# An fp32 first layer by 20 block products in four PSUM banks in place of 22 in pairs of banks

## The chip, the cores and the metric

The kernel runs on one core of a Trainium2 chip. The time is device time in microseconds (us) of one launch; three runs of the kernel before gave 584.62, 584.01 and 584.42, median 584.42. Engines are named TensorE (PE, matmul; PEld is its weight load), VectorE (DVE), ScalarE (ACT), GpSimd (POOL) and SyncE (SP, which here only issues DMAs). Every engine works off its own instructions in the order in which the program wrote them.

## The reference

An RWKV-6 attention over a sequence of 768 steps, and then a two-layer network with a silu between the layers. All arrays are float32.

```python
B, H, S, D = r.shape                    # 4, 8, 768, 48
for t in range(S):
    cur = einsum('bhd,bhe->bhde', u * k[t], v[t])
    y[t] = einsum('bhd,bhde->bhe', r[t], state + cur)
    state = w[t][..., None] * state + einsum('bhd,bhe->bhde', k[t], v[t])
x = y.transpose(0, 2, 1, 3).reshape(B * S, H * D)      # 3072 x 384
h = x @ w_in                                           # w_in 384 x 2048
out = (h * sigmoid(h)) @ w_out                         # w_out 2048 x 384
```

## The kernel before

The 3072 tokens are cut into 12 units: 128 steps of two of the four batches, so a unit has 256 tokens of the network. `mix(i)` writes the attention of unit i as a list of groups of steps; the main loop walks the groups and puts after each one a number of steps of the network: the second layer of unit i - 2 (`downs`, seven products per unit by a Strassen-like scheme, called quarters here) and the first layer of unit i - 1 (`ups`). The schedule is manual: what this order says is the order on each engine's queue. After mix(11) follows a tail without attention: `downs(10)`, `ups(11)`, `downs(11)`.

Attention of a unit. `load_blocks(i, name, g)` loads a quarter of w, r or k with four small DMAs on SyncE's queue into `raw`; `turn` transposes it with VectorE; `product`, `grow_own`, `grow_keys` (GpSimd) and `grow_queries` (VectorE) build the scaled keys and queries level by level; `odd_keys` and half of `prepare` are ScalarE copies. `burst(i, l)` has TensorE make the scores of levels l and l + 1, and `keep_level` puts them into `score`: with VectorE for levels 3 and 4, with twelve ScalarE copies for levels 5 and 6. Scores inside blocks of eight steps go another way: `block_bonus` (GpSimd multiplications, steps 0 to 7) and `block_sum` (VectorE reductions, steps 0 to 4) fill `block_sums`; `block_move` sends them through DRAM (`kept`) back into `spare` in another layout, on SyncE's queue; `block_spread` copies that on ScalarE, and `block_write` writes it with two predicated copies of VectorE, each over a whole half of `score` (index e). At the unit's end `turn_apart`, `y_state`, `y_values` and `update` use `score` on TensorE, and `turns(i + 1)` transposes the next w and k. The result y goes through DRAM (`x_out`, `x_in`) into `xt`, the input of the first layer. `load_rk` loads the inputs of `block_bonus` for the next unit.

First layer, units 3 to 11. The transposed product has 2 x 3 x 2 blocks: w_in in two halves of its columns and three chunks of rows, x in three chunks of rows and two batches. 11 block products per half, made for two halves of 512 columns each (22 in all, each 8 matmuls of 64 weight columns by 128 tokens, recorded as 16 instructions), are accumulated in the banks h0, h1, o0 and o1. In the places x, y and z a product can follow a product of its place at once; the partial sums leave by `nc.scalar.copy` and come back by `nc.vector.tensor_tensor` into `gt`, not into PSUM. The sums of weights (`in_weight_sums`, four sums of 1024 columns) are made once in mix(3) and mix(4), the five sums of x per unit by `sums_of_x`. Then `sums` (L1130, VectorE) makes what the second layer needs: eight additions of 512 columns per unit.

Places. `slot` keeps w and r of the units from 4 on in slot 0 of `raw` and k in two slots by turns, so k is loaded two units ahead; slot 1 of w and r holds sums of weights from mix(3) on.

Of the kernel before, what the change touches and what calls it, by code (L numbers as in the profile page):

```python
# [38 lines left out]
def kernel(  # L39
# [59 lines left out]
    def slot(i, name):  # L99

        return 0 if i >= NPAIR and name != "k" else i % NSLOT
# [387 lines left out]
    def block_bonus(i, step):  # L489
# [3 lines left out]
        if step == 0:  # L493
            ruk[i] = pt.tile([128, 2 * W], F32, name="ruk", bufs=1)
            mul(ruk[i], at_rk(R_AT, [1, 2 * W]), at_rk(K_AT, [1, 2 * W]))
        elif step == 1:
            have = ruk[i].rearrange("p (e s d) -> p e s d", e=2, s=BLK)
            mul(have, have, u_bc[:, 0:1][:, :, None, :].to_broadcast([128, 2, BLK, D]))
# [18 lines left out]
        else:  # L517
            e = step - 6
            to = (room_b, ruk[i])[e]
            mul(to.rearrange("p (k q d) -> p k q d", k=4, q=4), at_rk(K_AT + e * W, [D, 4], [0, 4], [1, D]),  # L520
                at_rk(R_AT + e * W + 4 * D, [0, 4], [D, 4], [1, D]))
# [35 lines left out]
    def block_write(i):  # L557

        shape = [128, NB, NP, L // BLK, BLK]
        for e in range(2):  # L560
            nc.vector.copy_predicated(out=score[:, i % NSC, e].rearrange("p (b q) (i s) -> p b q i s", b=NB, s=BLK),
                                      mask=block_mask[:, :, None].to_broadcast(shape),
                                      data=block_both[:, :, e::2][:, :, :, None, :].to_broadcast(shape))
# [300 lines left out]
    p_x = {}  # L864

    def x_products(i, b):

        if b == 0:
            xt[i] = pt.tile([128, KC, TU], F32, name="xt", bufs=1)
# [53 lines left out]
    def x_in(i, queue=nc.scalar):  # L923

        xt[i] = pt.tile([128, KC, TU], F32, name="xt", bufs=1)
        queue.dma_start(out=xt[i], in_=turned[i].rearrange("h d t -> (h d) t").rearrange("(c p) t -> p c t", p=128))
# [11 lines left out]

    late = []

    def mix(i):
# [15 lines left out]
        def start(j):  # L957
            return [*[(product, j, l) for l in range(1, NL)], (grow_own, j, 1)]

        end = [[*at(i > NFAST, (sums, i - 1, 0)), *at(ahead, *bonus_steps(i + 1, 0, 1, 2, 3))],  # L960
               [*at(i < len(units) - NB, (turn_apart, i), (turn_k, i)), (y_state, i), *both(y_values, i), *at(ahead, *turns(i + 1)),
                *at(i <= NFAST, (sums, i - 1, FH // 2 - 2)), *both(update, i), *at(not ahead, (move_x, i))]]
        if i < NPAIR:
# [9 lines left out]
                      [(burst, i, 5), (keep_level, i, 5), (keep_level, i, 6), (go_on, i, 6)], *end]  # L973
        else:
            groups = [[*both(turn, i, "r"), (grow_own, i, 0), (x_out, i - 1)],
                      [*start(i), *sum_steps(i, 0, 1), *bonus_steps(i, 4, 5), (x_in, i - 1)],
                      [(odd_keys, i, 2), (grow_keys, i, 2, False), (grow_queries, i, 2), *sum_steps(i, 2)],
                      [(prepare, i, 3), *bonus_steps(i, 6, 7)],
                      [(burst, i, 3), (keep_level, i, 3), *sum_steps(i, 3, 4), (block_move, i), *at(ahead, (load_rk, i + 1))],
                      [(keep_level, i, 4), (go_on, i, 4)],  # L980
                      [(prepare, i, 5), (reverse_v, i)],
                      [(block_spread, i), (block_write, i)],
                      [(burst, i, 5), (keep_level, i, 5), (keep_level, i, 6), (go_on, i, 6)], *end]

        loads = [*at(i >= NPAIR and ahead, *block_loads(i + 1, "w")), *at(i >= NPAIR - 1 and ahead, *block_loads(i + 1, "r")),
                 *at(i + NSLOT < len(units), *block_loads(i + NSLOT, "k"))]
# [3 lines left out]
        if i == NPAIR - 1:  # L990
            late.extend(loads[-2:])
            loads = loads[:-2]
        if i == NPAIR:
            groups[1] += late
            groups[3] += loads[:2]
            loads = loads[2:]

        behind = groups[8 if i < NPAIR else 5 if i == NPAIR else 2:][:4 if i + NSLOT >= len(units) else None]
        for at, group in enumerate(behind):
            group += loads[at * len(loads) // len(behind):(at + 1) * len(loads) // len(behind)]  # L1000
# [8 lines left out]
    def up(i, m):  # L1009
        p_h = ps.tile([128, 2, TU], F32, name="p_h", bufs=2)  # L1010
        for a in range(2):
            f = 2 * m + a
            for c in range(KC):
                nc.tensor.matmul(p_h[:, a, :], lhsT=w_in_sb[:, c, f * 128:(f + 1) * 128], rhs=xt[i][:, c, :],  # L1014
                                 start=(c == 0), stop=(c == KC - 1))
# [9 lines left out]
    HALF = DF // 2  # L1025
    whole_w = raw[:, 1].rearrange("p x b h d -> p x (b h d)")
    in_sums = [whole_w[:, WRK["r"]], const.tile([128, HALF], F32, name="in_sum"), whole_w[:, WRK["w"]]]
    a11, a12, a13 = (w_in_sb[:, c, 0:HALF] for c in range(KC))
    a21, a22, a23 = (w_in_sb[:, c, HALF:DF] for c in range(KC))
    x_sums = [spare[:, at + x * L:at + (x + 1) * L] for x in range(3)] + [const.tile([128, L], F32, name="x_sum")]  # L1030

    def in_weight_sums(which):
        out, one, two, op = ((in_sums[0], a21, a22, ALU.add), (in_sums[1], in_sums[0], a11, ALU.subtract),
                             (in_sums[2], a12, in_sums[1], ALU.subtract), (a21, a11, a21, ALU.subtract))[which]
        nc.vector.tensor_tensor(out=out, in0=one, in1=two, op=op)

    def sums_of_x(i):

        (b11, b12), (b21, b22), (b31, b32) = (tuple(xt[i][:, c, b * L:(b + 1) * L] for b in range(NB)) for c in range(KC))
        d1, d2, d4, d3 = x_sums  # L1040
        for out, one, two in ((d1, b12, b11), (d2, b22, d1), (b12, b22, b12), (d4, b21, d2), (d3, b31, b32)):
            nc.vector.tensor_tensor(out=out, in0=one, in1=two, op=ALU.subtract)
# [9 lines left out]
    def first_layer(i, half, *names):  # L1052

        (b11, b12), (b21, b22), (b31, b32) = (tuple(xt[i][:, c, b * L:(b + 1) * L] for b in range(NB)) for c in range(KC))
        d1, d2, d4, d3 = x_sums
        s1, s2, s4 = in_sums
        for name in names:
            place, first, last, pairs = {
                "p1": ("x", True, True, [(a11, b11)]), "p6": ("x", False, True, [(s2, d2)]), "p7": ("x", False, True, [(a21, b12), (a23, b32)]),
                "p4": ("x", False, True, [(a22, d4), (a23, d3)]), "p5": ("y", True, True, [(s1, d1)]),  # L1060
                "p3": ("y", False, True, [(s4, b22), (a13, b32)]), "p2": ("z", True, False, [(a12, b21)]),
                "n1": ("z", False, True, [(a13, b31)])}[name]
            p = kept[{"x": ("h0", "h1"), "y": ("o0", "h0"), "z": ("o1", "o1")}[place][half]][:].rearrange("p (q t) -> p q t", q=4)
            for n, (left, right) in enumerate(pairs):
                for q in range(4):
                    for h in (0, PD):
                        f = (4 * half + q) * 128 + h
                        nc.tensor.matmul(p[h:h + PD, q, :], lhsT=left[:, f:f + PD], rhs=right, start=first and n == 0 and q == 0,  # L1068
                                         stop=last and n == len(pairs) - 1 and q == 3, skip_group_check=True)

            def g(x, b):
                if (i, x, b, half) not in gt:
                    gt[i, x, b, half] = pt.tile([128, 4, L], F32, name="gt", bufs=FC // 2)
                return gt[i, x, b, half]
# [244 lines left out]
```

## Time and profile before

| what | value |
|---|---|
| median of three runs | 584.42 us |
| span of the profiled execution | 582.4 us (the page gives no other time for it) |
| first quarter of mix(4) to the tail, eight units | 169.58 to 522.96 us |
| tail | 522.96 to 582.4 us |
| TensorE L1068, first layer (16 instructions make a block product) | 274 ns each, pipelined |
| VectorE L1080, joins of the first layer | 0.68 us each |
| VectorE L1130, sums, two SBUF operands | 0.91 and 0.70 us on average |
| VectorE L561, block_write | 1.31 to 2.93 us, mean 1.52 |
| ScalarE L1077 / L1083 / L1085, copy and silu of 512 columns | 0.58 / 0.63 / 0.59 us |
| GpSimd L491, 768 / 384 columns | 1.83 to 2.30 / 1.15 to 1.23 us |
| SyncE L127, issue of one block load | 0.45 us in the median, 0.31 to 1.9 |

Times are us from the span's start. A row of the timeline has start, duration, engine, line, operation, output <- inputs, shape and count; in brackets stands the idle time before it and what ended it. Rows with a count merge instructions that follow each other. The chain is the sequence of work and waits that ended last.

### The profile page before, as it was taken

What the parts mean: (1) busy time and instruction counts of PE and PEld (TensorE: products, weight loads), DVE (VectorE), ACT (ScalarE), POOL (GpSimd) and SP (SyncE); (2) the same over time, 40 slices, a digit from 0 to 9 for tenths busy, and PEclk for the clock granted to TensorE, in tenths of its full rate; (3) what the DMA queues carried; (4) which work ended last, traced back from release to release, by engine and by line L of the source; (5) the groups of instructions that cost most, each with busy time, mean ns of one, the idle gap of its engine ahead of it and who ended that gap; (6) DMA issues with size and microseconds to landing.
All of it is one profiled execution on the core that took longest, in us unless ns stands there. A gap on an engine that the chain in (4) does not pass through costs nothing.

```text
span 582.4 us, 19225 instructions
## 1 busy us (share of the span) xinstructions
PE 572.0 (98%) x8070; PEld 534.0 (92%) x8070; DVE 433.9 (75%) x703; ACT 264.4 (45%) x582; POOL 350.4 (60%) x415
## 2 busy tenths in 40 slices
PE   8989999999999999999999999999999999999997
PEld 7768776798899999999999999999999899999997
DVE  7979789998997787787787687697686877771150
ACT  5679694531531561561560560560471361471320
POOL 6989778447777459459457559559647847700000
PEclk9989999999999999999999999999999999999999
DMA  9957775344453544554545455545355462102000
GB/s 225 320 118 215 168 231 88 48 91 95 100 90 68 112 84 82 120 83 80 117 71 89 104 86 94 117 77 95 77 98 101 70 128 60 38 4 55 28 5 24
DMA packets 206102, 57.62 MB, mean 99 GB/s; under 512 B 185664, under 2 KB 197824, under 8 KB 206016
## 3 DMA queue, kind: packets, MB, share of 16 engines
q1 hardware_dynamic: 197904, 49.51, 42.1%
q10 hardware_dynamic: 8112, 6.88, 4.4%
q8 instruction: 63, 1.03, 0.8%
q14 instruction: 23, 0.19, 0.1%
HBM read 47.14 MB, written 9.18 MB: 97 GB/s over the span
## 4 chain that ended last, share of the span: by engine, by line
PE 81%; POOL 6%; DVE 6%; issue 3%; SPq 2%; DMA 1%; ACT 0%; DVEq 0%; POOLq 0%
PE p_o L1159 24%; PE p_h L1068 20%; PE p_o L1068 9%; PE p_h L1014 9%; PE p_h L1159 4%; PE p_m L1098 4%; PE p_sc L692 2%; POOL tk L634 2%; PE p_m L856 2%; PE p_m L835 2%; PE p_m L692 2%; SPq L127 1%; DVE score L710 1%; DMA raw<-in_r_dram 1%; POOL w_in_sb L259 1%
## 5 line engine op out<-in xcount | busy, mean ns | idle before, releaser
L634 POOL TENSOR_TENSOR tk<-tk,tw 128x256 f32<-128x256 f32 x128 | 89.8, 722 | 30.3 <-ACT tk L604 22.9
L1159 PE MATMUL p_o<-own,temps 128*128 128x192 f32 x528 | 87.9, 326 | 0.0
L1159 PEld LDWEIGHTS p_o<-own,temps 128*128 128x128 f32 x528 | 86.1, 190 | 0.1
L491 POOL TENSOR_TENSOR ruk<-tokens_rk 128x768 f32<-128x768 f32 (+1 forms) x32 | 54.3, 1707 | 44.8 <-DMA tokens_rk<-in_k_dram 35.2
L406 POOL TENSOR_TENSOR tw<-tw 128x256 f32<-128x256 f32 (+6 forms) x83 | 39.3, 473 | 54.4 <-DVE tw L360 50.5
L1014 PE MATMUL p_h<-xt,w_in_sb 128*128 128x256 f32 x288 | 67.8, 391 | 0.8 <-POOL w_in_sb L259 0.6
L1014 PEld LDWEIGHTS p_h<-xt,w_in_sb 128*128 128x128 f32 x288 | 54.7, 194 | 9.3 <-POOL w_in_sb L259 1.1
L1068 PE MATMUL p_h<-xt,w_in_sb 128*64 128x128 f32 x1008 | 62.0, 274 | 0.0
L616 DVE TENSOR_TENSOR tr<-tr,tw 128x512 f32<-128x512 f32 x61 | 58.1, 953 | 3.0 <-PE p_m L692 2.5
L1159 PE MATMUL p_o<-w_out_sb,gt 128*128 128x192 f32 x340 | 60.0, 329 | 0.3 <-DVE temps L1130 0.2
L1159 PEld LDWEIGHTS p_o<-w_out_sb,gt 128*128 128x128 f32 x340 | 55.3, 190 | 1.5 <-DVE temps L1130 0.5
L1068 PEld LDWEIGHTS p_h<-xt,w_in_sb 128*64 128x64 f32 x1008 | 55.3, 137 | 1.3 <-issue 0.2
L604 ACT COPY tk<-tk 128x256 f32<-128x256 f32 x52 | 21.2, 407 | 76.0 <-POOL tk L634 62.6
L1068 PE MATMUL p_o<-xt,w_in_sb 128*64 128x128 f32 x720 | 47.0, 273 | 0.0
L1164 ACT COPY partial<-p_o 128x192 f32<-128x192 f32 x33 | 10.5, 319 | 78.5 <-PE p_o L1159 72.7
L1068 PEld LDWEIGHTS p_o<-xt,w_in_sb 128*64 128x64 f32 x720 | 40.9, 137 | 0.0
L1077 ACT COPY gt<-p_h 128x512 f32<-128x512 f32 x45 | 26.2, 583 | 31.1 <-PE p_h L1068 31.1
L710 DVE COPY_PREDICATED score<-mask,p_sc 128x512 f32<-128x512 int8 x42 | 31.3, 800 | 9.5 <-PE p_sc L692 9.2
L1083 ACT ACTIVATE gt<-gt 128x512 f32<-128x512 f32 x36 | 22.7, 631 | 31.6 <-DVE gt L1080 31.2
L525 DVE TENSOR_REDUCE block_sums<-ruk 128x4 f32<-128x192 f32 (+1 forms) x48 | 24.2, 546 | 15.0 <-POOL ruk L491 15.0
L1080 DVE TENSOR_TENSOR gt<-p_o,gt 128x512 f32<-128x512 f32 x27 | 18.5, 684 | 20.0 <-PE p_o L1068 20.0
L1159 PE MATMUL p_o<-w_out_sb,temps 128*128 128x192 f32 x176 | 30.4, 326 | 0.0
(225 smaller groups left out, 1236.3 us busy)
## 6 DMA issues: line engine op xcount, KB each, us to landing
w_out_sb<-in_moe_w_in_dram SPq DMA_DIRECT2D x6, 768.0 KB, 6.7
w_out_sb<-in_moe_w_out_dram SPq DMA_DIRECT2D x4, 768.0 KB, 5.0
own<-in_moe_w_out_dram SPq DMA_DIRECT2D x4, 768.0 KB, 5.7
tokens_rk<-in_r_dram SPq DMA_DIRECT2D x8, 384.0 KB, 4.5
tokens_rk<-in_k_dram SPq DMA_DIRECT2D x8, 384.0 KB, 5.3
tokens_w<-in_w_dram SPq DMA_DIRECT2D x8, 384.0 KB, 6.8
turned<-yt ACTq DMA_DIRECT2D x16, 192.0 KB, 2.7
xt<-turned ACTq DMA_DIRECT2D x8, 384.0 KB, 3.3
```

The costliest lines, as they stand in the source:

```text
L406: engine.tensor_tensor(out=up, in0=t[:, :, 0::2], in1=t[:, :, 1::2], op=ALU.mult)
L491: mul = lambda out, one, two: nc.gpsimd.tensor_tensor(out=out, in0=one, in1=two, op=ALU.mult)
L525: add = lambda out, have: nc.vector.tensor_reduce(out=out, in_=have, axis=mybir.AxisListType.X, op=ALU.add)
L616: nc.vector.tensor_tensor(out=odd, in0=odd, in1=tw[i][l][:, :, 0::2][:, :, :, None].to_broadcast([128, Q, L >> (l + 1), c]), op=ALU.mult)
L634: nc.gpsimd.tensor_tensor(out=out, in0=have, in1=odd_products(i, l, b, *blocks), op=ALU.mult)
L692: nc.tensor.matmul(to, lhsT=tk[i][rows, X[l % 2] + p, x * 64:(x + 1) * 64], rhs=have, start=True, stop=True)
L710: nc.vector.copy_predicated(out=dst, mask=masks[l][:, :, None].to_broadcast([128, NB, NP, ni, c]), data=sc[e].rearrange("p (b q) (i c) -> ...
L1014: nc.tensor.matmul(p_h[:, a, :], lhsT=w_in_sb[:, c, f * 128:(f + 1) * 128], rhs=xt[i][:, c, :], start=(c == 0), stop=(c == KC - 1))
L1068: nc.tensor.matmul(p[h:h + PD, q, :], lhsT=left[:, f:f + PD], rhs=right, start=first and n == 0 and q == 0, stop=last and n == len(pairs) ...
L1077: nc.scalar.copy(out=g(*{"p1": (0, 0), "p6": (0, 1), "p5": (1, 1)}[name]), in_=p)
L1098: nc.tensor.matmul(po[i, b], lhsT=gt[i, f // 2][:, f % 2, b * L:(b + 1) * L], rhs=w_out_sb[:, f, :], start=(f == 0), stop=(f == FC - 1))
L1159: nc.tensor.matmul(p, lhsT=left(f), rhs=right[:, f, :], start=which in (0, 1, 3) and f == 0, stop=f == FH - 1, skip_group_check=True)
```

## The change

The first layer from unit 3 on is cut finer: w_in in four quarters of 512 columns, so the product has 4 x 3 x 2 blocks, and 20 block products in place of 22 give it. Each of four banks holds a running sum. Between products the content of a bank is copied to another bank or to `gt`, or joined with such a copy and written back into a bank, and the next product is added onto it (`ORDER`, `first_part`). Each product is a step of its own in `ups`.

21 sums of weights of 512 columns replace four of 1024, on VectorE and GpSimd in mix(3) and mix(4); they use all of slot 1 of `raw`, so k has one slot from unit 4 on and is loaded one unit ahead. The sums of x are eight instructions in eight numbered steps, with a room of two more rows in `xt` and one `gt` buffer.

`mix` has more and smaller groups, each with its own number of network steps; what VectorE does in them is spread anew, block_bonus step 5 is behind prepare(i, 3), block_spread behind burst(i, 5), and block_write is cut in two groups. The loads of the next unit have fixed places: w and k and the values in the first three groups, r one block at a time in the groups 4 to 7, of which group 7 also has block_move and load_rk. GpSimd's products over 768 columns in steps 0, 1, 6 and 7 are cut in two of 384. All sums for the second layer now read `gt` in SBUF.

```diff
     def slot(i, name):
-        return 0 if i >= NPAIR and name != "k" else i % NSLOT
+        return 0 if i >= NPAIR else i % NSLOT
...
         if step == 0:
             ruk[i] = pt.tile([128, 2 * W], F32, name="ruk", bufs=1)
-            mul(ruk[i], at_rk(R_AT, [1, 2 * W]), at_rk(K_AT, [1, 2 * W]))
+            for e in range(2):
+                mul(ruk[i][:, e * W:(e + 1) * W], at_rk(R_AT + e * W, [1, W]), at_rk(K_AT + e * W, [1, W]))
...
         else:
-            groups = [[*both(turn, i, "r"), (grow_own, i, 0), (x_out, i - 1)],
-                      [*start(i), *sum_steps(i, 0, 1), *bonus_steps(i, 4, 5), (x_in, i - 1)],
-                      [(odd_keys, i, 2), (grow_keys, i, 2, False), (grow_queries, i, 2), *sum_steps(i, 2)],
-                      [(prepare, i, 3), *bonus_steps(i, 6, 7)],
-                      [(burst, i, 3), (keep_level, i, 3), *sum_steps(i, 3, 4), (block_move, i), *at(ahead, (load_rk, i + 1))],
-                      [(keep_level, i, 4), (go_on, i, 4)],
-                      [(prepare, i, 5), (reverse_v, i)],
-                      [(block_spread, i), (block_write, i)],
-                      [(burst, i, 5), (keep_level, i, 5), (keep_level, i, 6), (go_on, i, 6)], *end]
+            j = i - 1
+            groups = [([*both(turn, i, "r"), (grow_own, i, 0), (x_out, j)], 2),
+                      ([*start(i), *bonus_steps(i, 4), (x_in, j), (reverse_v, i)], 1),
+                      ([(odd_keys, i, 2), (grow_keys, i, 2, False), (grow_queries, i, 2), (sums_of_x, j, 0, 1, 2), *sum_steps(i, 2)], 2),
+                      ([(prepare, i, 3), *bonus_steps(i, 5, 6, 7), (sums_of_x, j, 3, 4, 5, 6)], 2),
+                      ([(burst, i, 3), (keep_level, i, 3)], 2),
+                      ([*sum_steps(i, 3)], 1),
+                      ([], 1),
+                      ([*sum_steps(i, 4), (block_move, i), *at(ahead, (load_rk, i + 1)), (keep_level, i, 4)], 2),
+                      ([(go_on, i, 4)], 1),
+                      ([], 2),
+                      ([], 1),
+                      ([(sums_of_x, j, 7)], 1),
+                      ([(prepare, i, 5)], 2),
+                      ([], 1),
+                      ([(burst, i, 5), (block_spread, i), (keep_level, i, 5), (keep_level, i, 6), (go_on, i, 6)], 1),
+                      ([(block_write, i, 0)], 2),
+                      ([(block_write, i, 1)], 1),
+                      (end[0], 2), (end[1], 0)]
...
+        elif ahead:
+            blocks = block_loads(i + 1, "wkr")
+            for at, some in ((0, blocks[0:3]), (1, blocks[3:6]), (2, [*blocks[6:8], (load_values, i + 1)]),
+                             (4, blocks[8:9]), (5, blocks[9:10]), (6, blocks[10:11]), (7, blocks[11:])):
+                groups[at][0].extend(some)
...
+    A_AT, B_AT, C_AT, D_AT = "h1", "h0", "o1", "o0"
+    ORDER = {20: (A_AT, True), 18: (C_AT, True), 14: (D_AT, True), 13: (A_AT, False), 2: (C_AT, False), 15: (C_AT, False),
+             4: (D_AT, False), 7: (B_AT, False), 19: (A_AT, False), 16: (C_AT, False), 1: (D_AT, False), 12: (B_AT, False),
+             9: (C_AT, False), 11: (A_AT, False), 3: (D_AT, False), 6: (D_AT, False), 10: (B_AT, False), 5: (A_AT, False),
+             8: (C_AT, False), 17: (D_AT, False)}
+
+    def first_part(i, n):
+        first_layer(i, n)
...
+        if n == 20:
+            copy(pb, pa)
+        elif n == 18:
+            copy(g(*u11), pc)
+        elif n == 14:
+            copy(g(*s32), pd)
+        elif n == 13:
+            join(pd, g(*u11), pa, ALU.subtract)
+        elif n == 15:
+            silu(1, 1, pc)
+        elif n == 4:
+            copy(pc, pd)
+        elif n == 7:
+            nc.scalar.activation(out=g(*s42), in_=pb, func=AF.Copy, scale=-1.0)
+            join(pb, pb, g(*s32), ALU.add)
+        elif n == 19:
+            join(g(*s42), g(*s42), pa, ALU.add)
+        elif n == 16:
+            copy(g(*v22), pc)
+        elif n == 1:
+            join(g(*s32), g(*s32), pd, ALU.subtract)
+            silu(3, 2, g(*s32))
+            join(pa, pa, g(*v22), ALU.add)
+        elif n == 9:
+            silu(2, 2, pc)
+        elif n == 11:
+            copy(g(*w21), pa)
+            join(pc, pb, g(*u11), ALU.subtract)
+            join(pb, pb, g(*w21), ALU.subtract)
+        elif n == 6:
+            silu(1, 2, pd)
+        elif n == 10:
+            join(pd, g(*s42), pb, ALU.add)
+            silu(4, 1, pb)
+        elif n == 5:
+            silu(2, 1, pa)
+        elif n == 8:
+            silu(3, 1, pc)
+        elif n == 17:
+            silu(4, 2, pd)
...
     def ups(i):
         if i >= NFAST:
-            made = [[(first_layer, i, half, name) for half, name in step] for step in order]
+            made = [[(first_part, i, n)] for n in ORDER]
             if i == len(units) - 1:
-                made[6].append((sums, i, 0))
+                made[10].append((sums_of_x, i, 7))
+            made[17].append((sums, i, 0))
             made[-1].append((sums, i, 1))
             return made
```

In a unit the second layer's seven quarters fall into the first four groups; the products 20 and 18 follow burst 3, product 3 follows burst 5, and 8 and 17 are the last.

## The prediction

> **What bounds the kernel now.** I read the page's busy times and its chain first.
>
> ```profile
> span 582.4 us, 19225 instructions
> PE 572.0 (98%) x8070; PEld 534.0 (92%) x8070; DVE 433.9 (75%) x703; ACT 264.4 (45%) x582; POOL 350.4 (60%) x415
> PE 81%; POOL 6%; DVE 6%; issue 3%; SPq 2%; DMA 1%; ACT 0%; DVEq 0%; POOLq 0%
> ```
>
> TensorE carries the time and four fifths of the chain. The next view cuts the span at the first second-layer product of successive units.
>
> ```profile
> core 0: us, PE busy (x) PEld busy (x) DVE busy (x) ACT busy (x) POOL busy (x), PEclk, DMA share, GB/s
> 347.30:391.76 44.46, 44.46 (x722) 43.39 (x721) 35.80 (x56) 19.46 (x48) 30.83 (x35) 1.00 0.51 95
> 391.76:436.00 44.24, 44.24 (x721) 43.35 (x721) 33.81 (x56) 19.47 (x48) 29.57 (x35) 1.00 0.48 90
> ```
>
> TensorE has no idle time in a unit, at full clock (1.00); VectorE has 9 us free and ScalarE 25. In the chain, mix(4) starts at 169.58 and the tail at 522.96: eight units of 44.17 us, then 59.4 us. So the price of a product is next, in the timeline of TensorE.
>
> ```profile
> 366.72 1.09 PE L1068 MATMUL p_h<-xt,w_in_sb 128*64 128x128 f32 x16
> 367.65 1.04 PE L1068 MATMUL p_o<-spare,raw 128*64 128x128 f32 x16
> 368.52 1.04 PE L1068 MATMUL p_o<-xt,w_in_sb 128*64 128x128 f32 x16
> ```
>
> One block product is a row of 16; from start to start it takes 0.87 us. Then what will stand around the products: SyncE's queue, ScalarE and VectorE in the same unit.
>
> ```profile
> 350.96 9.06 SPq L127 DMA_DIRECT2D raw<-in_k_dram  x16
> 360.12 3.85 SPq L127 DMA_DIRECT2D raw<-in_w_dram  x8
> 370.14 0.33 SPq L544 DMA_DIRECT2D kept<-block_sums  x1
> 371.68 1.00 SPq L547 DMA_DIRECT2D spare<-kept  x2
> ```
>
> SyncE needs 13.0 us to issue 24 block loads (0.54 each; 0.48 in the last eight), and it holds `kept` back until VectorE's block sums are ready (it idles before 370.14), so the two `spare` transfers are back early.
>
> ```profile
> 377.05 0.23 ACT L552 COPY spare<-spare 128x64 f32<-128x64 f32 x1
> 377.29 1.00 ACT L554 COPY spare<-spare 32x64 f32<-32x64 f32 x4
> 383.34 0.63 ACT L1083 ACTIVATE gt<-gt 128x512 f32<-128x512 f32 x1 [2.66 <-DVE gt L1080]
> 383.87 2.13 ACT L792 COPY score<-p_sc 32x128 f32<-32x128 f32 x8
> 386.03 1.51 ACT L792 COPY score<-p_m 64x256 f32<-64x256 f32 x4
> ```
>
> ScalarE obeys program order: its silu waited 2.66 us for a join that VectorE had behind block_write, and the twelve score copies stood behind that silu. TensorE didn't stop, because no product of this kernel needs what those instructions leave in PSUM so soon.
>
> ```profile
> 363.43 0.75 DVE L1042 TENSOR_TENSOR xt<-xt 128x128 f32<-128x128 f32 x1
> 364.11 0.28 DVE L1042 TENSOR_TENSOR spare<-xt,spare 128x128 f32<-128x128 f32 x1
> 378.59 4.15 DVE L561 COPY_PREDICATED score<-spare 128x1024 f32<-128x1024 int8 x2
> ```
>
> The same subtraction took 0.28 us alone and 0.75 us beside GpSimd; block_write's pair took 4.15 us here and 2.52 us in the unit before.
>
> **The change, part by part.** The sum goes against this execution: span 582.4 us. The page gives no time beyond the span; the median of the runs, 584.42, is 2.0 us above it, and I take these 2.0 as unchanged.
>
> *Products.* 22 become 20 in nine units: 2 x 0.873 = 1.75 us of TensorE each, or 15.7 us in all. Eight units lie in mix(4) to mix(11), one in the tail. A unit without waits would be 42.42 us.
>
> *Joins and seeds.* Per unit VectorE gets eight joins for six (+1.4 us at 0.68), eight sums of x for five (these took 3.1 us; between 8 x 0.28 = 2.2 and 8 x 0.75 = 6.0, I take 5.5 because GpSimd is busy at that place), and ScalarE seven copies for six (+0.58). In 9 us of free VectorE this costs nothing by itself; without that cover it would be some 4 us a unit. But now products are summed onto what a join or a copy left, so each seed is a wait of TensorE, and these I follow in order. From the unit's start: 7 second-layer products 18.4, burst 3 to 19.5, then 0.873 each and burst 5 (1.09) before product 3. Product 11 starts at 30.84; it needs the second join behind product 1 (result at 29.30, two joins, 30.6): in time by 0.2. Products 4, 12, 16 and 10 have 0.8 us or more. Burst 5 needs GpSimd's keys behind a ScalarE copy that is queued behind the silu of product 1: ready at 32.2 for 32.2. I cost all these at nothing; 0.5 at most.
>
> Product 17 is different. It needs the join that overwrites bank D, and that needs ScalarE's silu of bank D behind product 6. In program order ScalarE's silu stands behind block_spread (1.24), keep_level 5 (2.13) and keep_level 6 (1.51). ScalarE is done with product 11's copy at 32.5: +1.24 +2.13 +1.51 +0.59 = 38.0, the join 0.7, so 17 starts at 38.8. TensorE is there at 37.17 (only products 3, 6, 10, 5, 8 lie between). That is a wait of 1.6 us. VectorE's first block_write stands before that join and must wait for keep_level 6 of the same half of `score` (done 36.65): with 1.3 us it ends in time, with 2.1 us the wait is 2.35. I take 2.0, the middle. Behind 17 on TensorE stand turn_apart and the unit's y: all of it moves. The unit is 44.4 us, against 44.17.
>
> *SyncE.* The change moves the k loads of the next unit into this one and puts all w and k loads (32 DMAs), the values (5), two outputs and three of the four r blocks (12) ahead of block_move. The first w load overwrites what turn(i, "w") reads, so it waits for VectorE's transposes at the unit's start. block_move's transfers feed block_spread, which stands before everything just listed on ScalarE; VectorE's block_write, its eight sums and then turn(i+1, "w") close a ring. Once around: 32 x 0.54 = 17.3; values 2.5 (343.06 to 345.60); outputs 0.75; r 12 x 0.48 = 5.8 (nothing else is in flight then); `kept` to the landing of `spare` 1.54 + 0.5 + 2.5 = 4.5; ScalarE 5.5; join 0.7; second block_write 1.5; sums 8 x 0.69 = 5.5; transposes 1.2. Sum 45.3 us, so the ring and not TensorE sets the unit: +1.1 us in each of the seven units that load for a next one (mix(4) to mix(10)), +7.9. The ends: with 0.48 a load, 1.9 for values, 4.0, 1.3 and sums of 0.6 it is 41.2, and the wait of 2.0 decides; with 0.57, 3.7, r at 0.67 and the dearer VectorE rows it is 52. I stay near the rows of the unit shown. What it removes: the r blocks landed up to 2.8 us late at a unit's start; worth 0.2 a unit, already in the 44.17 as mean, and covered by the ring.
>
> mix(11) loads nothing: -1.75 + 2.0 = +0.2.
>
> *GpSimd.* Multiplications of 768 columns (1.83) become two of 384 (1.15 to 1.2 each): four more instructions, some 2 us a unit in 14 us of idle time: nothing. Bonus step 5 (2.7) now stands behind the keys of level 3, which ended only at 18.3 for a burst at 18.4: room for 2.7.
>
> *Weight sums, once.* mix(3): on VectorE three of 1.2 become six of 0.68: +0.5, and VectorE has 42.55 of 45.75 busy there. Five on GpSimd in idle time: nothing. mix(4): three on GpSimd (1.2 to 1.4 each, from the 384-wide row and 512 columns) ahead of the keys of level 3: 3.9 less the room of 2.7 = +1.2 (0 to 4.2).
>
> *Tail.* -1.75; the first second-layer product of the last unit starts in bank D behind 17 and its silu: 0.9 idle where 0.24 is now. -1.1.
>
> Sum: 7.9 + 0.2 + 0.5 + 1.2 - 1.1 = +8.7: span 591.1, time 593.
>
> **A rule on the shared port.** Of the eight sums for the second layer (L1130) four have an operand in PSUM now (0.68 each) and none will; the rows of that line with two SBUF operands have means of 0.70 and 0.91. The Trainium skill, SBUF — State Buffer, Who interferes with whom, says that a VectorE instruction with two SBUF inputs and a GpSimd instruction that reads SBUF exclude each other for a whole instruction. The trace agrees where the subtraction went from 0.28 to 0.75 us. By the rule the unit would be that of the second rival below; by the rows alone it is 45.3.
>
> **The rivals.** *SyncE is in time.* If a load costs 0.48, block_move comes before ScalarE asks for it; only the wait before 17 is left: 8 x 0.25 + 0.5 + 1.2 - 1.1 = +2.6, 587 (584 to 590 for waits of 1.6 to 2.35). For it: eight loads did take 3.85. Against: 24 took 13.0.
>
> *VectorE and GpSimd block each other.* The bonus products of the next unit follow load_rk, which now stands behind block_move, so they meet block_write and the sums. With sums of 0.91 (+1.8) and 2.1 for a block_write (+0.6) the ring is 47.7: 7 x 3.5 + 0.8 = +25.5, 610. For it: the 4.15 us row. Against: the splits shorten each block.
>
> *The products are gained (the other side).* If ScalarE reaches bank D's silu while product 8 still runs, there is no wait: 8 x -1.75 + 0.5 + 1.2 - 1.1 = -13.4, 571. For it: ScalarE is 45% busy. Against: 5.5 us of its work in a row against 4.4 us of products. It decides from a wait under 1.75 us a unit, and with half of that it is 578.
>
> **How the numbers follow.** Forecast 0.42 (589 to 600), SyncE in time 0.20, blocking 0.14, products gained 0.24. A change under 0.2% (1.2 us) can't be told from none. Faster 0.24; same 0.04, the lower end of the second case; slower 0.72. The range leaves out the ends of both outer cases: 573 to 606.
>
> **What would show it.** Units of about 45.3 us. TensorE idle 2 to 3 us before product 17, released by VectorE's join; ScalarE idle before the first copy of block_spread, released by the DMA of `spare`; SyncE's queue full from the transposes to block_move. If TensorE idles elsewhere (before 11 or burst 5), my queue orders are wrong; if it has no idle time, the third rival holds; if block_spread waits for nothing, the ring is not closed.

## The result and the profile after

The changed kernel takes 633.75 us (633.63 to 636.27), the kernel before beside it 584.52: a ratio of 1.0828, 95% interval 1.0784 to 1.0871. The forecast was 593 with 573 to 606 as its range; the direction was right and the size was not. The profiled execution has a span of 634.2 us, 51.8 more than before; it is the slowest of the four, with a time of 636.27, so the time lies 2.1 us above its span, as the prediction took it (2.0).

The page's busy times and its chain:

```profile
span 634.2 us, 18828 instructions
PE 579.4 (91%) x7782; PEld 535.3 (84%) x7782; DVE 484.8 (76%) x753; ACT 268.1 (42%) x591; POOL 391.8 (62%) x459
PE 54%; DVE 13%; ACT 9%; DMA 7%; SPq 6%; POOL 6%; issue 4%; DVEq 0%; POOLq 0%; ACTq 0%
```

TensorE's share of the chain fell from 81% to 54%. VectorE, ScalarE, DMAs, SyncE's queue and GpSimd share the rest; such a mixture fits a ring through all of them, but doesn't show one by itself. Two units, cut at the first second-layer product of each (us, then busy time by engine, granted clock, DMA share):

```profile
core 0: us, PE busy (x) PEld busy (x) DVE busy (x) ACT busy (x) POOL busy (x), PEclk, DMA share, GB/s
327.25:378.02 50.77, 46.48 (x693) 45.05 (x689) 40.11 (x61) 20.21 (x50) 32.59 (x39) 0.90 0.44 82
378.02:430.45 52.43, 45.42 (x692) 43.93 (x689) 39.42 (x61) 19.20 (x48) 32.60 (x39) 0.90 0.44 80
```

A unit takes 50.8 and 52.4 us where it took 44.2 to 44.5; the granted clock is 0.90 where it was 1.00. TensorE's timeline shows where it stops, and what follows:

```profile
363.75 1.04 PE L1135 MATMUL p_o<-xt,w_in_sb 128*64 128x128 f32 x16
369.09 1.98 PE L1135 MATMUL p_o<-xt,w_in_sb 128*64 128x128 f32 x16 [4.29 <-DVE p_o L1162]
370.99 1.09 PE L814 MATMUL p_sc<-ident,tk 48*128 48x48 f32 x16
372.01 1.98 PE L838 MATMUL p_m<-tr,state 48*48 48x128 f32 x32
...
422.63 1.97 PE L1135 MATMUL p_o<-xt,w_in_sb 128*64 128x128 f32 x16 [7.01 <-DVE p_o L1162]
```

The first row is product 8, the second is product 17, held 4.29 us for VectorE's join; in the next unit it is 7.01, and in mix(5) to mix(10) it is never less than 4.29. After the wait TensorE is slow: product 17 takes 1.98 us for 1.04 to 1.09 elsewhere. SyncE's queue in that unit:

```profile
330.03 7.86 SPq L127 DMA_DIRECT2D raw<-in_w_dram  x16
338.00 7.80 SPq L127 DMA_DIRECT2D raw<-in_k_dram  x16
...
350.04 6.90 SPq L127 DMA_DIRECT2D raw<-in_r_dram  x12
357.04 0.40 SPq L547 DMA_DIRECT2D kept<-block_sums  x1
360.22 1.01 SPq L550 DMA_DIRECT2D spare<-kept  x2
...
381.24 2.79 SPq L127 DMA_DIRECT2D raw<-in_w_dram  x6
```

The queue issues without a pause from 330.03 to `kept` at 357.04; the next unit's first load comes at 381.24, 51.2 us after this unit's. Between the two stand ScalarE, VectorE and GpSimd, one timeline each:

```profile
362.51 0.24 ACT L555 COPY spare<-spare 128x64 f32<-128x64 f32 x1 [2.69 <-DMA spare<-kept]
367.70 0.60 ACT L1159 ACTIVATE gt<-p_o 128x512 f32<-128x512 f32 x1
```

```profile
368.33 0.70 DVE L1162 TENSOR_TENSOR p_o<-gt,p_h 128x512 f32<-128x512 f32 x1
368.94 2.11 DVE L564 COPY_PREDICATED score<-spare 128x1024 f32<-128x1024 int8 x1
370.94 2.89 DVE L1249 TENSOR_TENSOR temps<-gt 128x512 f32<-128x512 f32 x2
373.76 1.48 DVE L1249 TENSOR_TENSOR temps<-temps,gt 128x512 f32<-128x512 f32 x1
375.34 1.30 DVE L1249 TENSOR_TENSOR temps<-gt,temps 128x512 f32<-128x512 f32 x1
...
379.91 1.29 DVE L360 STREAM_TRANSPOSE tw<-raw 128x512 f32<-128x512 f32 x2
```

```profile
368.88 3.00 POOL L491 TENSOR_TENSOR ruk<-tokens_rk 128x384 f32<-128x384 f32 x2 [9.29 <-DMA tokens_rk<-in_k_dram]
371.84 2.85 POOL L491 TENSOR_TENSOR ruk<-ruk,u_bc 128x384 f32<-128x384 f32 x2
```

ScalarE waits for the transfer, the join waits for ScalarE's silu, and the sums (L1249) take 9.0 us, because GpSimd's bonus products start in the same microseconds.

Where the 51.8 us are, with the starts of the units read from the same product rows in both traces:

| stretch | before | after | difference | predicted |
|---|---|---|---|---|
| to mix(3)'s first quarter | 120.97 | 121.2 | +0.2 | 0 |
| mix(3) | 48.44 | 56.2 | +7.8 | +0.5 |
| mix(4) | 44.34 | 45.7 | +1.4 | +2.3 |
| mix(5) to mix(10), six units | 266.3 | 309.0 | +42.7 | +6.6 |
| mix(11) | 42.84 | 43.84 | +1.0 | +0.2 |
| tail | 59.5 | 58.2 | -1.3 | -1.1 |

### The profile page after: what moved, and what is told of

The parts are those of the page before. It is cut to its first block, busy times and chain, and to the rows that moved or that the text cites. A ratio compares the mean times of both kernels' runs of the same rounds, so it can differ in the third digit from the quotient of the medians.

```text
span 634.2 us, 18828 instructions
## 1 busy us (share of the span) xinstructions
PE 579.4 (91%) x7782; PEld 535.3 (84%) x7782; DVE 484.8 (76%) x753; ACT 268.1 (42%) x591; POOL 391.8 (62%) x459
## 4 chain that ended last, share of the span: by engine, by line
PE 54%; DVE 13%; ACT 9%; DMA 7%; SPq 6%; POOL 6%; issue 4%; DVEq 0%; POOLq 0%; ACTq 0%
PE p_o L1278 19%; PE p_o L1135 7%; PE p_h L1028 6%; ACT score L795 5%; SPq L127 4%; PE p_h L1135 4%; PE p_m L1217 3%; PE p_h L1278 3%; PE p_m L859 3%; DMA spare<-kept 3%; PE p_m L838 2%; DMA kept<-block_sums 2%; POOL tk L637 2%; DVE tr L619 2%; PE p_sc L695 2%
## 5 line engine op out<-in xcount | busy, mean ns | idle before, releaser
L1135 PE MATMUL p_o<-xt,w_in_sb 128*64 128x128 f32 x1152 | 79.5, 286 | 36.0 <-DVE p_o L1162 35.7
L1135 PEld LDWEIGHTS p_o<-xt,w_in_sb 128*64 128x64 f32 x1152 | 69.0, 144 | 38.2 <-DVE p_o L1162 37.6
L491 POOL TENSOR_TENSOR ruk<-tokens_rk 128x384 f32<-128x384 f32 x48 | 59.4, 1259 | 60.3 <-DMA tokens_rk<-in_k_dram 60.3
L1249 DVE TENSOR_TENSOR temps<-gt 128x512 f32<-128x512 f32 (+1 forms) x48 | 47.4, 1025 | 2.3 <-ACT gt L1037 2.3
L619 DVE TENSOR_TENSOR tr<-tr,tw 128x512 f32<-128x512 f32 x61 | 48.5, 795 | 0.5
L1159 ACT ACTIVATE gt<-p_o 128x512 f32<-128x512 f32 x45 | 26.6, 598 | 23.2 <-PE p_o L1135 23.0
L564 DVE COPY_PREDICATED score<-spare 128x1024 f32<-128x1024 int8 x16 | 22.9, 1434 | 15.9 <-ACT score L795 15.9
L864 ACT COPY yt<-p_m 48x512 f32<-48x512 f32 x40 | 23.2, 580 | 22.6 <-PE p_m L859 22.0
L1278 PEld LDWEIGHTS p_o<-w_out_sb,temps 128*128 128x128 f32 x176 | 28.7, 190 | 1.7 <-ACT partial L1283 1.7
L1278 PE MATMUL p_h<-w_out_sb,gt 128*128 128x192 f32 x168 | 29.1, 326 | 0.0
```

What stands on the lines that cost most here:

```text
L491: mul = lambda out, one, two: nc.gpsimd.tensor_tensor(out=out, in0=one, in1=two, op=ALU.mult)
L619: nc.vector.tensor_tensor(out=odd, in0=odd, in1=tw[i][l][:, :, 0::2][:, :, :, None].to_broadcast([128, Q, L >> (l + 1), c]), op=ALU.mult)
L1159: nc.scalar.activation(out=g(f, t), in_=have, func=AF.Silu)
L1278: nc.tensor.matmul(p, lhsT=left(f), rhs=right[:, f, :], start=which in (0, 1, 3) and f == 0, stop=f == FH - 1, skip_group_check=True)
```

## The experiments

Two causes were in dispute for the six units: the ring through SyncE's queue, or the order of ScalarE's and VectorE's queues ahead of product 17 (block_spread, keep_level and block_write before a silu and a join). The second place to explain was mix(3).

**The loads behind block_move.** The values and all r blocks are issued after `block_move` and `load_rk`; everything else is the changed kernel. (In the runs below, line numbers differ by a few from one kernel to the next.)

```diff
-for at, some in ((0, blocks[0:3]), (1, blocks[3:6]), (2, [*blocks[6:8], (load_values, i + 1)]),
-                 (4, blocks[8:9]), (5, blocks[9:10]), (6, blocks[10:11]), (7, blocks[11:])):
+for at, some in ((0, blocks[0:3]), (1, blocks[3:6]), (2, blocks[6:8]), (7, [(load_values, i + 1), *blocks[8:]])):
```

> The changed kernel, with the values and the four r blocks issued behind block_move and load_rk; w and k stay ahead of it. Theory 'ring' (SyncE's loads ahead of block_move close a loop of 51 us through block_spread, the score copies, block_write, the sums and the transposes): block_move is back before ScalarE asks for it, the units fall from 51.2 to 44.4 us if TensorE keeps its clock over a wait of 2 us, or to 48 if the clock drops as it does now: 593 to 613 us in all. Theory 'seed' (the wait before product 17 is made by ScalarE's copies and VectorE's block_write whatever SyncE does): units stay at 50 or more, 630 to 634 us.

600.85 us, ratio 1.0252 (1.0237 to 1.0268), span 598.9: 35 us less from the order of 17 DMAs. The units of mix(5) to mix(10) take 45.2 us on average (271.1 for six). A unit, the wait before 17 in it, and SyncE there, in three views of this kernel:

```profile
316.03:361.08 45.05, 43.19 (x693) 41.47 (x689) 38.65 (x61) 19.66 (x49) 32.79 (x39) 1.00 0.52 95
```

```profile
355.97 1.09 PE L1134 MATMUL p_o<-xt,w_in_sb 128*64 128x128 f32 x16 [1.34 <-DVE p_o L1161]
```

```profile
328.17 9.11 SPq L127 DMA_DIRECT2D raw<-in_k_dram  x16
...
341.98 0.33 SPq L547 DMA_DIRECT2D kept<-block_sums  x1
343.52 1.00 SPq L550 DMA_DIRECT2D spare<-kept  x2
```

SyncE is now free before `kept` and waits for the block sums. `spare` is issued 1.54 us after `kept`, as in the kernel before; in the changed kernel it took 3.2 us in the unit shown. (That is no rule for loads in flight: in mix(4) to mix(10) it took 1.6 to 3.5 us there, four times of seven no more than 1.65, and here, to mix(11), six times of eight 1.5 and twice 2.3 and 2.6.) The wait of product 17 in mix(5) to mix(10) is 1.2 to 1.7 us, at full clock (1.00). So the ring was closed, and it was the cause of most of the loss.

**ScalarE's and VectorE's order alone.** The loads stay as in the changed kernel; the copies into `score` and both block_writes go behind the silu of product 6 and the join behind product 10.

```diff
-([(burst, i, 5), (block_spread, i), (keep_level, i, 5), (keep_level, i, 6), (go_on, i, 6)], 1),
-([(block_write, i, 0)], 2),
-([(block_write, i, 1)], 1),
+([(burst, i, 5)], 1),
+([], 2),
+([(block_spread, i), (keep_level, i, 5), (keep_level, i, 6), (go_on, i, 6), (block_write, i, 0), (block_write, i, 1)], 1),
```

> The changed kernel with its loads as they are, but block_spread, the score copies of levels 5 and 6 and both block_writes written behind the silu of product 6 and the join of product 10, so that product 17's seed stands ahead of them on ScalarE and VectorE. Theory 'ring': the loop is as long as before, only the place of TensorE's wait moves from product 17 to the unit's y; 628 to 636 us. Theory 'seed': the wait and the low clock behind it go, 7 us in each of six units: about 590 us.

643.71 us, 1.0987 (1.0970 to 1.1003): not a gain, but 10 us more than the changed kernel, and 8 above the range given for a ring. Product 17 no longer waits; the two instructions behind it do (TensorE's timeline, turn_apart):

```profile
371.12 0.23 PE L814 MATMUL p_sc<-ident,tk 48*128 48x48 f32 x1 [1.61 <-ACT score L795]
372.12 0.69 PE L814 MATMUL p_sc<-ident,tk 48*128 48x48 f32 x15 [0.77 <-ACT score L795]
```

A ring is not shortened by a new order of two of its links: what was ahead of the join is now ahead of the unit's y, and the loads of the next unit still wait for all of it. From the first w load of a unit to that of the next it takes 51.7 us on average, with this edit and without it. Most of what is lost stands in mix(4) (+3.4 us) and mix(11) (+5.3), where product 17 had waited only 0.94 and 1.15 us; the expectation left these units out. With this diff and the one of the loads together:

> Both edits together. Theory 'ring' and theory 'seed' in turn: with the loop opened (first edit) the wait of 2 us before product 17 is what is left, and the second edit trades it for a wait before the unit's y of 0 to 3 us: units of 43 to 45.5 us, 583 to 600 us in all. If the second edit gains nothing over the first, the seed was never worth more than y's wait; if the sum is that of the second edit alone, the loop was not the cause.

624.38 us, 1.0655 (1.0622 to 1.0688), 24 us above the range and 23.5 more than with the loads alone, for the same reason: TensorE waits 10.6 us for score copies in turn_apart and 7.3 in the first matmuls of y_state behind it. The order ahead of product 17 was not the cause.

**The loads alone, in the kernel before.** The 22 products, the groups and the waits of the kernel before, with k in one slot and all loads in the order of the changed kernel.

```diff
-        return 0 if i >= NPAIR and name != "k" else i % NSLOT
+        return 0 if i >= NPAIR else i % NSLOT
...
+            blocks = block_loads(i + 1, "wkr")
+            for at, some in ((0, blocks[0:3]), (1, blocks[3:6]), (2, [*blocks[6:8], (load_values, i + 1)])):
+                groups[at] += some
+            groups[4][3:3] = blocks[8:11]
+            groups[4] += blocks[11:]
```

> The kernel before, with one part of the change alone: k in one slot, and w, k, the values and three r blocks of the next unit ahead of block_move. Theory 'ring': the loop also goes through this kernel (block_move, block_spread, block_write, the joins, score copies, silus, sums, transposes): seven units grow by 3 to 6 us, 605 to 625 us. Theory 'seed': this kernel seeds no bank from a join, so nothing changes: 584 to 587 us.

627.01 us, 1.0698 (1.0680 to 1.0716): +41 us with none of the new products, 2 us above the range. ScalarE's and TensorE's timelines in one unit:

```profile
405.08 0.24 ACT L552 COPY spare<-spare 128x64 f32<-128x64 f32 x1 [4.21 <-DMA spare<-kept]
```

```profile
407.81 1.97 PE L1066 MATMUL p_h<-spare,raw 128*64 128x128 f32 x16 [4.89 <-ACT gt L1083]
```

The same delay, found by the first instruction of this kernel that needs ScalarE; from first w load to first w load a unit takes 51.0 us here and 51.7 in the changed kernel. So the six slow units owe their length to the place of the loads and not to the scheme of products.

**The clock after the wait.** In the changed kernel 40 small matmuls with zero weights are added onto bank C behind product 8, to fill the wait; they add nothing to the sums.

```diff
         elif n == 8:
+            if i < len(units) - 1:
+                for x in range(5):
+                    for q in range(4):
+                        for h in (0, PD):
+                            nc.tensor.matmul(pc[h:h + 16, q, :], lhsT=none, rhs=right_of[i, 8], start=False, stop=q == 3, skip_group_check=True)
             silu(3, 1, pc)
```

> The changed kernel, with 40 matmuls of a zero weight (16 columns) added onto bank C behind product 8, so that TensorE works instead of waiting before product 17 in the units 3 to 10; the sum is unchanged by them. If the low clock behind the wait (product 17 in 1.98 us, y's first matmuls in 1.98 for 1.13) is only a result of the wait, the units stay at 50 to 51.5 us because the ring sets them, and product 17 takes 1.0 us: 628 to 637 us. If the slow stretch is itself on the path, 3.5 us go in each of six units: about 612 us. If the clock stays low although TensorE worked, it is not the idle time that lowers it.

638.96 us, 1.0929 (1.0867 to 1.0991): no gain over 1.0828, and 2 us above the range given for a ring. Product 17 and what follows run at full rate (TensorE's timeline):

```profile
315.56 4.55 PE L1208 MATMUL p_o<-xt,none 128*16 128x128 f32 x80
320.03 1.09 PE L1137 MATMUL p_o<-xt,w_in_sb 128*64 128x128 f32 x16
```

So the slow clock is a result of the wait. The profiled span is 634.2 us, the same as without the filling, but that is a coincidence of two sums: mix(5) to mix(10) take 298.9 us for 309.0, while mix(11), with no ring and little wait to fill, takes 5.1 us more, mix(4) 2.7, and what stands ahead of it 2.3. A unit of the six gains 1.7 us, neither nothing nor 3.5, and from first w load to first w load it takes 50.9 us for 51.7: the ring still sets the unit, and the slow clock is a small part of the loss.

The Trainium skill (TensorE: Matmul & The Clock Gate, What's actually happening) says that the array falls to half rate after an idle window of about 3.4 us. The traces agree for long waits: rows behind 4.29, 4.89 and 7.01 us took 1.97 to 1.98 us, the one behind 1.34 us took 1.09. They don't agree with 3.4 us as the least. In the run with a quarter moved ahead (below), 16 matmuls of the second layer behind waits of 1.94 and 2.74 us, from TensorE's timeline:

```profile
333.22 2.87 PE L1278 MATMUL p_o<-w_out_sb,gt 128*128 128x192 f32 x16 [1.94 <-DVE ob L1286]
424.71 4.28 PE L1278 MATMUL p_o<-w_out_sb,gt 128*128 128x192 f32 x16 [2.74 <-DVE ob L1286]
```

The second row starts at a granted clock of 0.50.

**mix(3): GpSimd beside VectorE.** In the changed kernel TensorE waits 6.08 us in mix(3) for a silu that stands behind score copies, and these wait for VectorE's bonus_write. TensorE, VectorE and GpSimd there:

```profile
166.43 4.26 PE L1028 MATMUL p_h<-xt,w_in_sb 128*128 128x256 f32 x12 [6.08 <-ACT gt L1037]
```

```profile
155.33 1.23 DVE L583 COPY both_b<-diag 128x16 f32<-128x16 f32 x1
156.57 2.47 DVE L585 COPY both_b<-diag 32x16 f32<-32x16 f32 x4
...
159.32 3.77 DVE L593 COPY_PREDICATED score<-own_mask,both_b 128x1024 f32<-128x1024 int8 x2
```

```profile
155.21 1.32 POOL L1074 TENSOR_TENSOR raw<-in_sum,raw 128x512 f32<-128x512 f32 x1
156.61 1.26 POOL L1074 TENSOR_TENSOR raw<-raw,w_in_sb 128x512 f32<-128x512 f32 x1
```

A copy of 16 columns takes as long as a GpSimd sum beside it. In the kernel before GpSimd idled from 151.8 to 155.8 us, and the same rows were:

```profile
151.78 0.16 DVE L580 COPY both_b<-diag 128x16 f32<-128x16 f32 x1
151.96 0.71 DVE L582 COPY both_b<-diag 32x16 f32<-32x16 f32 x4
152.94 2.50 DVE L590 COPY_PREDICATED score<-own_mask,both_b 128x1024 f32<-128x1024 int8 x2
```

First GpSimd's five sums were put behind the keys of level 6 (group 10), on top of the new order of loads:

```diff
-(7, nc.gpsimd, ("q14", "q3")), (8, nc.vector, ("q12a", "q12")), (9, nc.gpsimd, ("q", "n13", "t"))):
+(8, nc.vector, ("q12a", "q12")), (10, nc.gpsimd, ("q14", "q3", "q", "n13", "t"))):
```

> The first edit (values and r behind block_move) and, in mix(3), the five GpSimd sums of weights behind the level-6 keys. Units as with the first edit alone (45.2 us). If these GpSimd sums delay the keys, the block mask, bonus_write, the score copies and the silu that an up step waits for 6.3 us, mix(3) falls from 57.9 to about 50 us: 593 us. If VectorE's own sums of weights are the cause: 600 us.

603.20 us, 1.0290 (1.0264 to 1.0317): no gain over 600.85. I had thought that the keys came late; but the sums, from 152.0 to 158.9 us, still ran beside the same copies. Then they went to the end of group 11, behind the bonus products:

```diff
-(10, nc.gpsimd, ("q14", "q3", "q", "n13", "t"))):
+(11, nc.gpsimd, ("q14", "q3", "q", "n13", "t"))):
```

> Loads as in e1; GpSimd's five weight sums of mix(3) now stand behind its bonus products (group 11), where it idles from 167 to 171 us in e1. Theory: mix(3) is long because GpSimd works beside VectorE's small copies and its predicated copy (in the kernel before GpSimd idled from 151.8 to 155.8 us, while VectorE did just these); then the copies L585 go back from 2.5 to about 0.8 us, bonus_write starts at 153 to 155 us instead of 159 and mix(3) falls from 57.9 us to 50 to 53: span 591 to 594. Rival: VectorE's own six weight sums do it; then bonus_write is as late as in e1, mix(3) stays at 56 to 58 and the span at 597 to 600.

597.68 us, 1.0200 (1.0184 to 1.0216), span 596.0, 2.9 less than with the loads alone and 2 above the range. VectorE's and TensorE's timelines of this run:

```profile
153.08 0.17 DVE L583 COPY both_b<-diag 128x16 f32<-128x16 f32 x1
153.26 0.71 DVE L585 COPY both_b<-diag 32x16 f32<-32x16 f32 x4
...
154.25 2.49 DVE L593 COPY_PREDICATED score<-own_mask,both_b 128x1024 f32<-128x1024 int8 x2
```

```profile
181.07 8.88 PE L1277 MATMUL p_o<-own,temps 128*128 128x192 f32 x36 [3.65 <-DVE temps L1248]
```

The copies have the durations of the kernel before, and mix(3) takes 48.5 us instead of 57.9: the theory of the stretched copies holds, VectorE's own weight sums cost nothing visible. But mix(4) went from 45.7 to 52.2. GpSimd's sums now stand from 164.4 to 171.5 us, beside VectorE's sums for the second layer, and TensorE waits 3.65 us for those; the 36 matmuls behind that wait then take 8.88 us, at a granted clock of 0.50 up to 185 us (48 of them took 7.96 us in a unit of the changed kernel). Seven tenths of that gain moved on to the next place where the two engines meet. The Trainium skill (SBUF — State Buffer, Who interferes with whom) says that copies and casts too, in the modes that use both of VectorE's ports, and not only instructions with two SBUF inputs, can hold and wait for the port shared with GpSimd, for a whole instruction. The rows of 1.23 against 0.16 us agree.

**What bounds a unit of 45.2 us.** On top of the loads and the weight sums behind group 10, ScalarE's keep_level 6 goes behind the silu of product 6, and both block_writes go behind the join.

```diff
-([(burst, i, 5), (block_spread, i), (keep_level, i, 5), (keep_level, i, 6), (go_on, i, 6)], 1),
-([(block_write, i, 0)], 2),
-([(block_write, i, 1)], 1),
+([(burst, i, 5), (block_spread, i), (keep_level, i, 5)], 1),
+([], 1),
+([(keep_level, i, 6), (go_on, i, 6)], 1),
+([(block_write, i, 0), (block_write, i, 1)], 1),
```

> As before this, and the score copies split: block_spread and level 5 stay behind burst 5, level 6 comes behind the silu of product 6, both block_writes behind the join of product 10. By the queues product 17 then waits for nothing (its join at 39.6 for 39.5) and y waits 0.3 us for the second block_write: units of 43.7 to 44.2 us, 580 to 586 us. If y or turn_apart wait for the copies as with both edits of the first set (48 us a unit): 595 us or more.

601.72 us, 1.0264 (1.0230 to 1.0298), for 580 to 586 expected. Product 17 doesn't wait any more, yet a unit still takes 45.3 us. TensorE's list of waits in the units of this run (us in total, times, longest):

```profile
PE p_o L1278 <- ACT partial L1283: 8.1, 7, 1.7
PE p_m L845 <- DVE score L564: 4.2, 5, 1.7
```

The waits stand in the second layer's quarters and at the unit's y instead. With one quarter more in the second group and one less in the third:

```diff
-([*start(i), *bonus_steps(i, 4), (x_in, j), (reverse_v, i)], 1),
-([(odd_keys, i, 2), ..., (sums_of_x, j, 0, 1, 2), *sum_steps(i, 2)], 2),
+([*start(i), *bonus_steps(i, 4), (x_in, j), (reverse_v, i)], 2),
+([(odd_keys, i, 2), ..., (sums_of_x, j, 0, 1, 2), *sum_steps(i, 2)], 1),
```

> As before this, and one quarter moved ahead: fourth quarter's copy no longer stands behind odd_keys of level 2 on ScalarE. The quarters took 19.45 us for 18.4 in a unit with the first edit; half to all of that goes: 0.5 to 1.0 us in each of seven units, 573 to 582 us. If the quarters' waits come from VectorE's joins instead, nothing changes.

606.97 us, 1.0348 (1.0307 to 1.0388), for 573 to 582 expected: the waits now end with VectorE's join of a quarter (12.7 us over seven units), and it is slower. So VectorE was tested by taking work from it:

```diff
             e = step - 3
+            if i > NPAIR:
+                return
             add(at_sums(e * E + 4, ...
```

> Built on f2_split_copies; from the sixth unit on VectorE leaves out the two block sums of steps 3 and 4 (0.95 us each), so block_sums keeps old values there and part of the scores inside blocks is not computed. Theory: once the waits for SyncE and for product 17 are gone, VectorE's order sets the unit of 45.3 us (38.5 busy, with short waits between); then the units from the sixth on fall by 1 to 1.9 us, to 43.4 to 44.3, and the span by 6 to 12, to 586 to 592. Rival: ScalarE's copies of partial sums or GpSimd set it; then the units stay within 0.4 us of 45.3 and the span at 596 to 600.

590.68 us, 1.0080 (1.0062 to 1.0099), span 589.8. Five units, mix(6) to mix(10), of the run with all its block sums and of the one without two:

```profile
269.59:496.08 226.49, 215.03 (x3396) 206.87 (x3392) 193.18 (x301) 96.37 (x237) 161.85 (x195) 1.00 0.51 92
```

```profile
270.31:489.49 219.18, 213.61 (x3397) 206.85 (x3393) 176.59 (x289) 96.27 (x237) 153.56 (x195) 1.00 0.52 95
```

A unit falls from 45.3 to 43.8 us, so VectorE's queue is on the path. How much of that is VectorE's own work stays open: the two reductions of 0.95 us carried with them a wait of 1.4 us a unit for GpSimd's products, which is gone as well; the eight sums for the second layer take some 1.5 us less a unit, because four of them went from 1.07 us on average to 0.68; and GpSimd's busy time fell by 1.7 us a unit beside it. Last, the loads behind block_move, the weight sums in group 11 and the split of the copies into `score`, together (no line is new):

> h1_weight_sums_last together with the split of f2_split_copies (keep_level 6 behind the silu of product 6, block_write behind the join after product 10). If the two gains are separate: 0.9 us under h1's span, 590 to 593, still above the kernel before by 1.3 to 2%. If VectorE's order is what is left, the units stay at 45.2 and the whole stays within 1 us of h1.

596.95 us, 1.0191 (1.0175 to 1.0206), within 1 us of h1: the split adds nothing while VectorE's order is what is left. This is the best complete version that I found, and it still takes 1.9% more than the kernel before: of the 12.8 us in the span, mix(4) has 7.5 and the six units behind it 4.9.

## Why the prediction was wrong, and where it was right

*Products.* Right: product starts lie 0.87 us apart, and the tail fell by 1.3 us (predicted 1.1).

*The place of the wait.* Right: in mix(5) to mix(10) there is none before 11, before burst 5 or at the other seeds (mix(4) has one of 0.96 us before 11); TensorE reached product 17 37.4 us into the unit (predicted 37.17) and waited for VectorE's join. Without the ring that wait is 1.2 to 1.7 us, at or under the low end of 1.6 to 2.35, and I had taken 2.0.

*The ring.* The mechanism was right; the step that failed is its size, 45.3 us, where the trace has 51.2, and in that sum above all the term of the eight sums, 5.5 us, where 9.0 were paid:

| link | predicted | measured, unit of 327.25 |
|---|---|---|
| loads, values, outputs, r, up to `kept` | 26.35 | 27.0 |
| `kept` to ScalarE's first copy | 4.5 | 5.5 |
| ScalarE to the end of the silu | 5.5 | 5.8 |
| join | 0.7 | 0.6 |
| second block_write | 1.5 | 2.0 |
| eight sums | 5.5 | 9.0 |
| transposes | 1.2 | 1.3 |

3.5 of the 5.9 us are the sums, priced at their row alone although the second rival named what stands beside them. That rival had the mechanism, two engines that exclude each other, and also too small a price: 1.8 us for the sums where 3.5 were paid. The sums take 8.9 to 9.0 us in the other five units too; there the loads up to `kept` take 28.1 to 29.3 us, and the way to ScalarE's first copy 3.9 to 5.8. The row that had shown the exclusion was read too simply: the subtraction of 0.28 us was not alone, it began together with a GpSimd product (364.11 to 364.89 us). On a ring every such microsecond is paid in each unit: 6 x 5.9 = 35.4 of the 43.1 us that the forecast of the span missed.

*mix(3).* "Five on GpSimd in idle time: nothing" failed: +7.8 us for +0.5. I had looked at whether GpSimd was idle, and not at what VectorE did in that time, small copies for which bonus_write, the score copies, a silu and TensorE wait in turn.

*mix(4).* +1.4 us for +2.3 is near in part by luck: the 1.1 us that the ring was to cost in this unit was not paid, since it takes 45.7 us with the loads in either place.

*Joins and sums in 9 us of free VectorE "cost nothing".* Wrong, though hidden behind the ring: with the ring open a unit is 45.2 and not 44.4 us. VectorE's busy time of 38.6 us was near what my terms add up to, but 6 us of free time in an engine that waits in program order for four others is no cover.

*The third rival.* It said that without the wait before 17 the products would be gained. The run without that wait has units of 45.3 us: it needed a second condition, room on VectorE, that I had not stated.

*The range.* It was built from the ends of single terms. The high end of the ring, 52, was on record, and seven units at 52 would have given 7 x 7.8 + 0.8 = 55 us; I closed the range at 606, by the blocking rival's 610, and left that end out.

## What to carry to other kernels

When a change puts loads ahead of a transfer that the same unit needs, write down the whole ring, from the load that waits for a buffer back to the reader that frees it, and price each link in the company that it will have, since every microsecond is paid once per round. Idle time of GpSimd is not free where VectorE has copies, predicated copies or sums of two SBUF operands in it, the forms that grew here: ask what VectorE does in those microseconds, and who waits for that. When a wait is taken away and the time stays, look where the next wait ends before another order is tried.

## What was not expected of the hardware

A VectorE copy of 128 x 16 took 0.16 us with GpSimd idle and 1.23 beside a GpSimd sum of 1.32 us; four of 32 x 16 went from 0.71 to 2.47 us. Two predicated copies of 128 x 1024 went from 2.50 to 3.77 us. TensorE's granted clock was 0.50 behind idle stretches of 4.3 us and more, but also behind one of 2.74 us, and 16 matmuls behind 1.94 us in the same run took their usual 2.87 us. Filling the waits brought the granted clock of five of the six units from 0.90 to 0.93 up to 1.00 and shortened the ring only from 51.7 to 50.9 us.
